# A table of rank offsets for the plan of the attention stage

## The chip, the cores and the metric

The kernel runs on 1 core of a Trainium2 chip. The metric is the device time of one execution in microseconds. The comparison is with the kernel before, whose median of 3 runs is 1107.73 us (1107.68 to 1110.07).

## What is computed

Attention over 2 batches, 8 heads, 576 positions and a head size of 64, then a gated product, then a soft mixture of eight experts, all in float32. Cut to what matters:

```python
q_rot, k_rot = rotate(q), rotate(k)                       # rotary embedding
attn = softmax(q_rot @ k_rot.T / sqrt(64))                # per batch and head
x = (attn @ v)  -> 1152 tokens x 512
x = ((x @ w1) * (x @ w2)) @ w3 @ w_out                    # w3 (1024x1024), w_out (1024x512)
P = sinkhorn(x @ w_gate)                                  # 8 rounds over rows and columns
out = sum over e of P[:, e] * (relu(x @ ew1[e]) @ ew2[e])
```

## The kernel before

Three stages follow each other. **Attention** fills the first 183 us or so; the heads are taken in eight pairs, n = 0 to 7. For each pair the rows of q and k are loaded (`load_qk`, tile `raw`), rotated (`rope_mul`, `rope_add`), cut into a high and a low part (`rope_hi` on ScalarE, `rope_lo`), and spread over partitions by transfers from SBUF to SBUF (`spread_k` into `kk`, `spread_q` into `sq`). Then come nine blocks of scores: four query tiles i = 0 to 3 with a block for each head (`scores`, L351) and one mixed block (`mixed_scores`, L374). A block's row maximum is taken on VectorE (`row_max`, L381), its exponential on ScalarE (`exponentials`, L385), its transposes on TensorE (`transposes`, L399 to L405, three or two groups of up to three), and these are copied from PSUM (`moved`, L418) by VectorE or ScalarE. `norm_columns` (L439, L442) turns the row sums, and `values` (L456) multiplies with v. Scores have two banks of PSUM (psS), transposes two (psT).

In the same stage the matrix product w3 @ w_out is made (`w34_product`, L242 to L244, three matmuls for each of 64 products; `w34_hi` L249 and `w34_lo` L254 take each finished i off its one bank psW). It doesn't depend on attention and fills TensorE where attention leaves it free. Its operands come as 64-bit words by eight loads of w_out (`wo_load`) and sixteen of w3 (`w3_load`, u = 0 to 15) into two buffers `wide`, and are converted in five steps: ScalarE to `cvy` (L193), VectorE shift (L198) and join (L201) to `cvu`, ScalarE high part (L206), and a low part on GpSimd or VectorE (L209). The high and low parts of w3 have two places that take turns. What is left of the 64 products runs behind the last `values`; the last eight (i = 7) are outside the plan.

**The gated product** (`branch`, L153 to L155) begins at 208.23 us, **the experts** run from there to the end in an order of their own plan.

What sets the order in the attention stage is `Plan` (L54). Each step has costs in us for the engines that can run it, a rank, the steps that it needs, and buffers that it takes or frees. `order()` walks a simulated time: among all steps that could start, the one with the lowest rank is issued, on the engine where it is ready. The ranks are written by hand (a pair's time t = n x 18 us, minus 30 for its rope, plus 3.6 for each tile, 1000 for the w34 products). Each engine then runs its list in that order and waits at its head; SyncE issues nearly all transfers. Where the plan leaves TensorE idle by more than some 0.7 us, and no `w34_product` has been issued yet, it emits filler matmuls on `ident` (L635), whose result nobody reads.

Of the kernel before, what the change touches and what calls it, by code (L numbers as in the profile page):

```python
# [19 lines left out]
P = 128  # L20
# [30 lines left out]
QSCALE = D**-0.5  # L51


class Plan:  # L54


# [12 lines left out]
    def step(self, name, costs, rank, run, needs=(), takes=(), frees=(), port=(), paired=False):  # L69


        self.steps[name] = costs, rank, run, list(needs), list(takes), list(frees), port, paired

    def order(self, window=None):
        todo, now, busy = dict(self.steps), 0.0, dict.fromkeys(self.SIGNAL, 0.0)
# [47 lines left out]
def attention_two_moes(ctx: ExitStack, tc: tile.TileContext, rope, qk, v, mw12, mw3t, mwo, wg, ew1, ew2, out):  # L123
# [359 lines left out]
    def step(f, args, costs, rank, needs=(), takes=(), frees=(), **kw):  # L483

        many = f in (rope_mul, rope_add, rope_lo, moved, x_lo)
        plan.step((f, *args), costs, rank, lambda e: f(*args, ENG[e]) if many else f(*args), needs, takes, frees, **kw)
# [9 lines left out]
        plan.step(("tab", c), {"act": 0.1}, -99.0 + c.start / S, lambda e, c=c: act.dma_start(tab[:, :, c], rope[:, :, c]))  # L496
    for n in range(NP):
        t = n * NQ * TILE
        step(load_v, (n,), {"sp": moving(4 * P * (NBLK + 1) * D)}, t - 40.0, takes=[("v", n)])
        ready = []  # L500
        for w in (1, 0):
            pieces = (every,) if n else halves if w else (slice(0, SF), slice(SF, S))
            for c in pieces:
                a, m = (n, w, c), c.stop - c.start
                r = t - 30.0 if n else -50.0 if c.start == 0 or w else -40.0
                r += 2 * (1 - w)
                rot = [("pool", on_pool)] * (n > 0) + [("dve", on_dve)] * (n < 2)
                tk = [("raw", (n, w))] if c.start == 0 else []
                step(load_qk, a, {"sp": moving(8 * P * m)}, t - 30.0 - w if n else -90.0 + c.start / S + 0.1 * (1 - w), takes=tk)
                step(rope_mul, a, {e: f(2 * m) for e, f in rot}, r, [(load_qk, *a), ("tab", halves[0]), ("tab", halves[c.stop > HS])], port=both)  # L510
                step(rope_add, a, {e: f(m) for e, f in rot}, r, [(rope_mul, *a)], port=both)
                tk = [(("sq", "kk")[w], n)] if n else []
                step(rope_hi, a, {"act": act_sb(m)}, r, [(rope_add, *a)], tk)
                fr = [("raw", (n, w))] if n == 0 and c is pieces[-1] else []
                cost = {"pool": on_pool(m)} if n and w else {"dve": on_dve(m)}
                step(rope_lo, a, cost, r, [(rope_hi, *a)], frees=fr, port=both)
            if n == 0:
                ready.append([(rope_lo, 0, w, c) for c in pieces])
                continue
            ready.append([(rope_lo, n, w, every)])  # L520
            for j, x in ((j, x) for j in range(2) for x in range(2)):
                if w:
                    for part, made in enumerate((rope_hi, rope_lo)):
                        step(spread_k, (n, j, x, part), {"sp": moving(4 * D * S)}, t - 30.0, [(made, n, 1, every)], frees=[("raw", (n, 1))])
                        ready[-1].append((spread_k, n, j, x, part))
                else:
                    needs = [((rope_hi, rope_lo)[x], n, 0, every)]
                    step(spread_q, (n, j, x), {"sp": moving(4 * D * S)}, t - 30.0, needs, frees=[("raw", (n, 0))])
                    ready[-1].append((spread_q, n, j, x))
        before = []  # L530
        for i in range(NQ):
            g, k, _ = group(i)
            r = t + i * TILE
            for j in range(2 - (i == MIX)):
                tk = [("psS", (n, i, j))]
                if j == 0:
                    tk += [("e", (n, i)), ("nm", (n, i))] + [("sm", (n, g))] * (k == 0)
                fr = [("kk", n), ("sq", n)] if n and i == MIX else []
                needs = ready[0] + (ready[1] if n or i * P >= SF else ready[1][:1]) + before
                if i < MIX:  # L540
                    made = scores, n, i, j
                    step(scores, (n, i, j), {"pe": 0.53 if n else 0.8}, r + j, needs, tk, fr)
                else:
                    made = mixed_scores, n
                    if n == 0:
                        for q in range(2):
                            step(mix_first, (q,), {"act": 0.2}, r, ready[1])
                        needs = needs + [(mix_first, 0), (mix_first, 1)]
                    step(mixed_scores, (n,), {"pe": 1.14 if n else 1.7}, r + j, needs, tk, fr)
                before = [made]  # L550
                step(row_max, (n, i, j), {"dve": 0.68}, r - 0.1, before)
                fr = [("psS", (n, i, j))] + [("nm", (n, i))] * (j or i == MIX)
                step(exponentials, (n, i, j), {"act": 0.73}, r, [(row_max, n, i, j)], frees=fr)
            r += 6.0
            parts = 3 - (i == MIX)
            for p in range(parts):
                needs = [(exponentials, n, i, min(p, 1) * (i < MIX))] + ([(transposes, n, i, p - 1)] if p else [(transposes, n, i - 1, 0)] if k else [])
                tk = [("psT", (n, i, p))] + ([(f"et{g}", n)] if k == p == 0 else [])
                step(transposes, (n, i, p), {"pe": 0.33}, r, needs, tk, [("e", (n, i))] if p == parts - 1 else [])
                m = 3 * (P if i < MIX else P - HD * p)  # L560
                step(moved, (n, i, p), {"act": act_ps(m), "dve": on_dve(m)}, r, [(transposes, n, i, p)], frees=[("psT", (n, i, p))])
        for g, tiles in enumerate(TILES):
            a, ng = (n, g), (G0, G1)[g]
            r = t + (tiles[-1] + 2.0) * TILE
            needs = [(exponentials, n, i, j) for i in tiles for j in range(2 - (i == MIX))]
            step(norm_sums, a, {"act": 0.2}, r, needs)
            step(norm_rows, a, {"dve": 0.12}, r, [(norm_sums, *a)])
            step(norm_spread, a, {"act": act_sb((4 + g) * D)}, r, [(norm_rows, *a)], [("rb", a)], [("sm", a)])
            step(norm_columns, a, {"pe": (0.24, 0.4)[g]}, r, [(norm_spread, *a)], [("psT", (*a, "r"))], [("rb", a)])
            step(norm_moved, a, {"act": act_ps(ng)}, r, [(norm_columns, *a)], [("r", a)], [("psT", (*a, "r"))])  # L570
            r += 1.1 * TILE
            for m, blocks in enumerate(VPARTS):
                parts = {(i, p) for i in tiles for t in blocks for p in (({0, 2}, {1})[t > 2] if i < MIX else {int(t > 2)})}
                needs = [(moved, n, i, p) for i, p in sorted(parts)] + [(load_v, n)]
                needs += [(values, n, g, m - 1)] if m else []
                last = m == len(VPARTS) - 1
                fr = [(f"et{g}", n)] + [("v", n)] * g if last else []
                step(values, (n, g, m), {"pe": len(blocks) * ng / 600}, r, needs, [("psX", a)] if m == 0 else [], fr, paired=True)
            step(x_scale, a, {"dve": on_dve(ng)}, r, [(values, n, g, len(VPARTS) - 1), (norm_moved, *a)], [("xs", a)], [("psX", a), ("r", a)])
            step(x_hi, a, {"act": act_sb(ng)}, r, [(x_scale, *a)])  # L580
            step(x_lo, a, {"pool": on_pool(ng), "dve": on_dve(ng)}, r, [(x_hi, *a)], frees=[("xs", a)], port=both)

    def wide_steps(load, u, got, rank, takes):

        step(load, (u,), {"sp": moving(8 * P * WU)}, rank - 20.0, takes=[("wide", (load, u))])

        parts = (
            ({"act": 0.57}, (), ["cvy"], ["wide"], ()),
            ({"dve": 0.37}, (), ["cvu"], ["wide"], both),
            ({"dve": 0.63}, (0, 1), [], ["cvy"], both),  # L590
            ({"act": act_sb(WU)}, (2,), [], [], ()),
            ({"pool": on_pool(WU), "dve": on_dve(WU)}, (3,), [], ["cvu"], both),
        )
        for k, (cost, before, tk, fr, port) in enumerate(parts):
            needs = [(load, u)] + [(load, u, p) for p in before]
            tk, fr = ([(p, (load, u)) for p in ps] for ps in (tk, fr))
            tk += takes if k == 3 else []
            plan.step((load, u, k), cost, rank, lambda e, k=k: got[u][2][k](*[ENG[e]][: k == 4]), needs, tk, fr, port)
# [806 lines left out]
```

## Time and profile before

| | us |
|---|---|
| median of 3 runs | 1107.73 (1107.68 to 1110.07) |
| the profiled execution, time | 1109.31 |
| its span, first to last instruction | 1107.5 |
| TensorE busy in the span | 1093.8 (99%) |
| VectorE, ScalarE, GpSimd busy | 797.7, 672.7, 323.2 |
| start of the gated product | 208.23 |

A busy TensorE isn't a TensorE that does needed work: the fillers are counted as busy. Between the span and the time of the same execution lie 1.81 us.

### The profile page before, as it was taken

The numbers are of one execution on the slowest core, as the hardware profiler recorded it, in microseconds if no ns is written. First come the engines' busy times: TensorE is split into PE (matmuls) and PEld (weight loads), VectorE is DVE, ScalarE is ACT, GpSimd is POOL, SyncE is SP. The second block draws the span as 40 slices with busy tenths as digits, with TensorE's granted clock in tenths as the row PEclk, the third lists the DMA queues.
The fourth block names the chain that finished last, engine by engine and source line by source line (L and its number), as shares of the span: only waits on it lengthen the run. The fifth ranks groups of instructions, "written<-read, shape, count | busy, mean of one in ns | idle before, by whom it ended". The sixth has DMA issues, their size and how long they took to land.

```text
span 1107.5 us, 21133 instructions
## 1 busy us (share of the span) xinstructions
PE 1093.8 (99%) x8185; PEld 1039.0 (94%) x8185; DVE 797.7 (72%) x1377; ACT 672.7 (61%) x1393; POOL 323.2 (29%) x289
## 2 busy tenths in 40 slices
PE   8999999999999999999999999999999999999998
PEld 7777777899999999999999999999999999999998
DVE  7887765854433688777876777778776787777876
ACT  5877775643322545667666666666656666666663
POOL 1656441000010101334333333324333333333311
PEclk9999999999999999999999999999999999999999
DMA  7776751530040435787878788778888688787824
GB/s 245 240 231 193 234 166 58 195 129 20 20 118 13 109 96 112 156 181 151 191 155 171 164 172 179 166 150 181 173 163 179 140 188 178 157 184 141 188 37 115
DMA packets 86308, 167.20 MB, mean 151 GB/s; under 512 B 9536, under 2 KB 50240, under 8 KB 86208
## 3 DMA queue, kind: packets, MB, share of 16 engines
q0 software_dynamic: 47632, 55.33, 32.1%
q1 hardware_dynamic: 38032, 109.94, 32.0%
q8 instruction: 64, 1.05, 0.4%
q10 hardware_dynamic: 544, 0.59, 0.2%
q14 instruction: 36, 0.29, 0.1%
HBM read 112.02 MB, written 2.36 MB: 103 GB/s over the span
## 4 chain that ended last, share of the span: by engine, by line
PE 79%; DVE 2%; DMA 0%; ACT 0%; issue 0%; DVEq 0%; SPq 0%
PE T L878 6%; PE T L880 6%; PE T L879 6%; PE zT L984 5%; PE zT L985 5%; PE zT L986 5%; PE s L153 3%; PE s L155 3%; PE s L154 3%; PE Q L878 3%; PE Q L880 3%; PE Q L879 3%; PE zQ L984 3%; PE zQ L986 3%; PE zQ L985 3%; PE A L878 2%
## 5 line engine op out<-in xcount | busy, mean ns | idle before, releaser
L752 POOL DMA_DIRECT2D sums<-sums x92 | 93.9, 1020 | 246.3 <-DMA sums<-sums 90.0
L1035 POOL DMA_DIRECT2D acc<-ztmp x87 | 107.0, 1233 | 134.4 <-ACT ztmp L1032 65.9
L984 PE MATMUL zT<-f,hf 128*128 128x256 f32 x496 | 141.1, 284 | 0.0
L985 PE MATMUL zT<-f,hf 128*128 128x256 f32 x496 | 140.3, 283 | 0.0
L986 PE MATMUL zT<-f,hf 128*128 128x256 f32 x496 | 140.3, 283 | 0.0
L752 POOL DMA_DIRECT2D sums<-in_ew_dram x46 | 41.0, 891 | 270.6 <-issue 119.1
L984 PEld LDWEIGHTS zT<-f,hf 128*128 128x128 f32 x496 | 94.8, 191 | 0.6
L986 PEld LDWEIGHTS zT<-f,hf 128*128 128x128 f32 x496 | 95.2, 192 | 0.0
L985 PEld LDWEIGHTS zT<-f,hf 128*128 128x128 f32 x496 | 94.9, 191 | 0.0
L148 DVE SCALAR_TENSOR_TENSOR y<-y 128x512 f32<-128x512 f32 x128 | 88.0, 687 | 2.3
L878 PE MATMUL T<-x,w 128*128 128x320 f32 x256 | 81.0, 316 | 0.0
L920 ACT ACTIVATE hf<-y 128x512 fp32r<-128x512 f32 x128 | 78.1, 631 | 2.7 <-DVE y L148 2.6
L148 DVE SCALAR_TENSOR_TENSOR hf<-y,hf 128x512 fp32r<-128x512 f32 x96 | 64.8, 686 | 20.2 <-ACT hf L918 20.1
L1032 ACT ACTIVATE ztmp<-ztmp,pr 128x256 f32<-128x256 f32 x174 | 78.6, 500 | 1.1 <-DVE ztmp L145 0.6
L880 PE MATMUL T<-x,w 128*128 128x320 f32 x256 | 79.1, 309 | 0.0
L879 PE MATMUL T<-x,w 128*128 128x320 f32 x256 | 79.0, 309 | 0.0
L918 ACT ACTIVATE hf<-y 128x512 fp32r<-128x512 f32 x96 | 60.1, 627 | 29.9 <-DVE y L889 25.7
L153 PE MATMUL s<-x,w 128*128 128x320 f32 (+1 forms) x256 | 76.2, 298 | 0.7 <-DVE gf L680 0.7
L155 PE MATMUL s<-x,w 128*128 128x320 f32 (+1 forms) x256 | 75.8, 296 | 0.0
L154 PE MATMUL s<-x,w 128*128 128x320 f32 (+1 forms) x256 | 75.8, 296 | 0.0
L878 PE MATMUL T<-y,w 128*128 128x256 f32 x256 | 72.5, 283 | 0.0
L880 PE MATMUL T<-y,w 128*128 128x256 f32 x256 | 72.4, 283 | 0.0
(308 smaller groups left out, 3695.6 us busy)
## 6 DMA issues: line engine op xcount, KB each, us to landing
sums<-in_ew_dram SPq DMA_DIRECT2D x62, 512.0 KB, 4.3
acc<-ztmp POOLq DMA_DIRECT2D x87, 256.0 KB, 5.6
wide<-in_ew_dram SPq DMA_DIRECT2D x34, 512.0 KB, 3.9
wide<-in_ew_dram SPq DMA_DIRECT2D x30, 384.0 KB, 5.2
wide<-in_mw3t_dram SPq DMA_DIRECT2D x16, 512.0 KB, 5.0
wide<-in_mw_dram SPq DMA_DIRECT2D x16, 512.0 KB, 3.2
sums<-in_ew_dram POOLq DMA_DIRECT2D x16, 512.0 KB, 6.5
sums<-sums POOLq DMA_DIRECT2D x32, 256.0 KB, 5.7
```

The lines of the kernel that those rows point to most:

```text
L148: dve.scalar_tensor_tensor(out=dst, in0=a, scalar=0.0, in1=b, op0=ALU.max, op1=op)
L153: pe.matmul(ps, wh, xh, start=(i == 0), stop=False)
L154: pe.matmul(ps, wh, xl, start=False, stop=False)
L155: pe.matmul(ps, wl, xh, start=False, stop=(i == n - 1))
L752: pool.dma_start(dst, src, accum_op=ALU.add)
L878: pe.matmul(ps, h[:, ws], x[0], start=(first and k == 0), stop=False, **kw)
L879: pe.matmul(ps, h[:, ws], x[1], start=False, stop=False, **kw)
L880: pe.matmul(ps, l[:, ws], x[0], start=False, stop=(k == 1), **kw)
L984: pe.matmul(ps[:, t], h, wh[:, u], start=(opens and u == 0), stop=False, **kw)
L985: pe.matmul(ps[:, t], h, wl[:, u], start=False, stop=False, **kw)
L986: pe.matmul(ps[:, t], l, wh[:, u], start=False, stop=(u == 1), **kw)
L1035: pool.dma_start(block(q, b, d), ztmp[:, slot(q, src)], accum_op=ALU.add)
```

## The change

A table `EARLIER` gives an offset for each kind of step and each pair n (or unit u); `Plan.step` adds it to the rank. Steps of the experts' plan have names that begin with a string and get none. The offsets are large against the hand-written ranks (up to some 2000), so inside what is ready they set a new order. The offsets come from a search over the plan itself, with durations scattered at random. Four added needs make buffers that are picked by number (`v`, the places of w3, `kk`, and the high parts of rope) be written in turn.

```diff
+EARLIER = dict(
+    scores=(-313, -222.5, -156.2, -1208.1, -593.3, -148.2, 765.3, 822.3,),
+    w34_product=(-626, 170.7, 528, -91.5, 296.2, 309.9, 683.5, 450.1, 404.3, -1426.6, -635, -452.7, 2110.7, -827.1,),
...
+def offset(name):
+    if isinstance(name[0], str):
+        return 0.0
+    f = name[0].__name__
+    i = name[1] if isinstance(name[1], int) else 0
...
+    return EARLIER.get(f, (0.0,) * (i + 1))[i]
...
-        self.steps[name] = costs, rank, run, list(needs), list(takes), list(frees), port, paired
+        self.steps[name] = costs, rank + offset(name), run, list(needs), list(takes), list(frees), port, paired
...
-        step(load_v, (n,), {"sp": moving(4 * P * (NBLK + 1) * D)}, t - 40.0, takes=[("v", n)])
+        step(load_v, (n,), {"sp": moving(4 * P * (NBLK + 1) * D)}, t - 40.0, [(load_v, n - 1)] if n else [], [("v", n)])
...
-                step(rope_hi, a, {"act": act_sb(m)}, r, [(rope_add, *a)], tk)
+                step(rope_hi, a, {"act": act_sb(m)}, r, [(rope_add, *a)] + ([(rope_hi, n - 1, w, every)] if n > 1 else []), tk)
...
+                        needs = [(made, n, 1, every)] + ([(spread_k, n - 1, 0, 0, 0)] if n > 1 else [])
...
+            needs = [(load, u)] + [(load, u, p) for p in before] + ([(load, u - 1, 3)] if takes and k == 3 and u else [])
```

No instruction of the needed work is added or removed. Line numbers of the changed kernel are higher by 43 or 44 (L399 is L442 there, L242 is L285, L635 is L679). From the gated product on, every engine has the same list in both kernels. In the attention stage the lists differ on all engines; the filler matmuls (L635) go from 48 to 41, of which the first 37 stand at the same places. Copies of transposes go from 59 on VectorE and 53 on ScalarE to 51 and 61. Of the 192 matmuls of the w34 products, 96 stood ahead of the last `values` and 111 do now.

TensorE, behind the mixed block (L374) of pair 2; before:

```order
L374 MATMUL s<-kk,sq_93 128x64
L399 MATMUL t<-ident,e 128x128 x6
L635 MATMUL w_105<-ident 128x128
L399 MATMUL t<-ident,e 128x128 x3
L635 MATMUL w_105<-ident 128x128 x5
L402 MATMUL t<-ident,e 128x128 x4
L405 MATMUL t<-ident,e 64x64 x2
L351 MATMUL s<-kk,sq_94 128x288 x8
```

TensorE at the same place, now:

```order
L417 MATMUL s<-kk,sq_93 128x64
L442 MATMUL t<-ident,e 128x128 x6
L285 MATMUL w_828<-y_85,y_86 128x512
L286 MATMUL w_828<-y_85,y_86 128x512
L287 MATMUL w_828<-y_85,y_86 128x512
...
L442 MATMUL t<-ident,e 128x128 x3
L394 MATMUL s<-kk,sq_94 128x288 x8
L445 MATMUL t<-ident,e 128x128 x4
L448 MATMUL t<-ident,e 64x64 x2
```

Six filler calls have gone and two w34 products (six matmuls, the row of dots is the second) stand in their place; the scores of pair 3 have moved ahead of the transposes of the mixed block.

VectorE, where the one bank of the w34 products is handed from one i to the next with the fewest TensorE instructions between; before, at pair 5, `keep` is the low part that frees the bank, `s` are scores, `t` transposes:

```order
L418 COPY et0_1554<-t_1587 128x3x128
L418 COPY et0_1554<-t_1593 128x3x128
L381 TENSOR_REDUCE nm_1600<-s_1602 128x1
L418 COPY et0_1554<-t_1615 128x3x128
L381 TENSOR_REDUCE nm_1600<-s_1624 128x1
L254 TENSOR_TENSOR keep_1632<-w34_1315,keep_1631 128x512
L418 COPY et0_1554<-t_1634 128x3x128
```

VectorE, the shortest such place now, at pair 3:

```order
L424 TENSOR_REDUCE nm_1117<-s_1118 128x1
L424 TENSOR_REDUCE nm_1117<-s_1127 128x1
L461 COPY et1_1155<-t_1162 128x3x128
L461 COPY et1_1155<-t_1171 128x3x128
L297 TENSOR_TENSOR keep_1177<-w34_828,keep_1176 128x512
L241 TENSOR_SCALAR cvu_1202<-wide_1124 128x512
L424 TENSOR_REDUCE nm_1180<-s_1181 128x1
```

The row maximum that stood between the copy and the low part now stands behind it. On TensorE, three transposes, four score matmuls and six transposes lay between the two products; now it is three transposes, a mixed block of ten matmuls and six transposes.

SyncE, the transfers ahead of the scores of pair 3 (`sq` is the query block), before:

```order
L322 DMA kk_800<-raw_656 64x576 x8
L312 DMA sq1_94<-raw_689 64x576
L314 DMA sq1_94<-raw_689 64x512
L315 DMA sq1_94<-raw_689 64x64
...
L180 DMA wide_911<-in_mwo_dram 128x1024
L180 DMA wide_927<-in_mw3t_dram 128x1024
```

SyncE, the same transfers now:

```order
L365 DMA kk_699<-raw_558 64x576 x8
L318 DMA raw_770<-in_qk_dram 128x1152
L355 DMA sq1_94<-raw_621 64x576 x2
L322 DMA v1_96<-in_v_dram 128x640
L223 DMA wide_825<-in_mw3t_dram 128x1024
L223 DMA wide_856<-in_mwo_dram 128x1024
L357 DMA sq1_94<-raw_621 64x512
L358 DMA sq1_94<-raw_621 64x64
```

Two loads into `wide` and one of v, which stood outside the six transfers of the query block, now stand between the first two and the last four. At pair 4 one such load stands between the first three and the last three.

## Rows read from the trace of the kernel before

**Rows 1.** The page, part 1: busy us (share), instructions of each engine.

```profile
PE 1093.8 (99%) x8185; PEld 1039.0 (94%) x8185; DVE 797.7 (72%) x1377; ACT 672.7 (61%) x1393; POOL 323.2 (29%) x289
```

**Rows 2.** Windows: stretch, its length, each engine's busy us (instructions), granted clock, DMA share, GB/s.

```profile
31.00:90.00 59.00, 56.99 (x434) 44.59 (x435) 47.76 (x86) 45.83 (x114) 37.31 (x23) 1.00 0.70 221
90.00:182.00 92.00, 89.31 (x638) 69.98 (x637) 66.90 (x121) 67.51 (x168) 36.43 (x22) 1.00 0.59 173
182.00:210.00 28.00, 27.38 (x135) 21.32 (x134) 17.73 (x30) 14.30 (x27) 5.27 (x4) 1.00 0.45 156
...
240.00:1107.00 867.00, 863.07 (x6581) 850.56 (x6579) 618.92 (x1058) 509.72 (x1010) 237.75 (x225) 1.00 0.66 140
```

**Rows 3.** Waits of TensorE, 31 to 210 us: total us, times, longest.

```profile
PE s L351 <- ACT e L385: 1.6, 4, 0.7
PE t L399 <- ACT et L418: 1.5, 4, 0.7
PE w L242 <- DVE keep L254: 0.7, 1, 0.7
PE t L244 <- POOL y L209: 0.6, 1, 0.6
PE t L402 <- ACT e L385: 0.4, 1, 0.4
PE t L399 <- DVE et L418: 0.3, 1, 0.3
PE s L351 <- DMA sq<-raw: 0.2, 1, 0.2
```

**Rows 4.** Timeline of TensorE, the fillers after 31 us: start, us, what [idle before].

```profile
31.80 0.39 PE L635 MATMUL w<-ident 128*128 128x128 f32 x2
32.53 0.79 PE L351 MATMUL s<-kk,sq 128*128 128x288 f32 x4 [0.34 <-ACT e L385]
...
51.93 0.49 PE L635 MATMUL w<-ident 128*128 128x128 f32 x2
52.72 0.80 PE L351 MATMUL s<-kk,sq 128*128 128x288 f32 x4 [0.30 <-ACT e L385]
...
60.39 0.83 PE L635 MATMUL w<-ident 128*128 128x128 f32 x6
61.51 0.55 PE L399 MATMUL t<-ident,e 128*128 128x128 f32 x3 [0.29 <-DVE et L418]
61.92 0.80 PE L351 MATMUL s<-kk,sq 128*128 128x288 f32 x4
...
68.63 0.39 PE L635 MATMUL w<-ident 128*128 128x128 f32 x2
...
69.42 1.28 PE L635 MATMUL w<-ident 128*128 128x128 f32 x10
71.05 0.66 PE L402 MATMUL t<-ident,e 128*128 128x128 f32 x4 [0.35 <-ACT e L385]
```

**Rows 5.** Timeline of TensorE, third group of nine transposes in a row, pair 3.

```profile
91.19 0.55 PE L399 MATMUL t<-ident,e 128*128 128x128 f32 x3 [0.75 <-ACT et L418]
```

**Rows 6.** Timelines of TensorE and VectorE at the bank's handover, pair 5.

```profile
126.11 0.49 PE L399 MATMUL t<-ident,e 128*128 128x128 f32 x3
126.35 0.78 PE L351 MATMUL s<-kk,sq 128*128 128x288 f32 x4
126.97 0.87 PE L399 MATMUL t<-ident,e 128*128 128x128 f32 x6
128.58 0.50 PE L242 MATMUL w<-y,y 128*128 128x512 f32 x1 [0.73 <-DVE keep L254]
...
127.17 0.76 DVE L381 TENSOR_REDUCE nm<-s 128x1 f32<-128x576 f32 x1
127.84 0.68 DVE L254 TENSOR_TENSOR keep<-w,keep 128x512 fp32r<-128x512 f32 x1
```

**Rows 7.** Waits of SyncE's queue, 31 to 180 us, for a free buffer `wide`.

```profile
SPq L180 <- DVE cvu L198: 29.2, 4, 18.2
```

More of the change, by code (lines that the diff above doesn't have):

```diff
@@ L51 @@
 QSCALE = D**-0.5
+EARLIER = dict(
+    tab=(-331.3,),
+    load_v=(-354.5, -305.2, -333.7, -395.2, -443.9, 51.4, 117.2, 192.7,),
+    load_qk=(-446.5, -563.6, -504.3, -521.9, -370.4, -480.6, -321.4, -369.9, -103.5, -302.6, 278.6, 84.4, 472.6, 406.8, 467.4, 843,),
+    rope=(1321.6, -520.9, -134.3, -274.1, 194.8, 7.4, -158.9, -290.5, 328.6, -520.8, 143.6, 402.5, 347.5, 45.1, 180.4, -275.3,),
+    scores=(-313, -222.5, -156.2, -1208.1, -593.3, -148.2, 765.3, 822.3,),
+    row_max=(95, -339.3, -459.3, -371.5, 64.3, 242.1, -463.7, -503.3,),
+    exponentials=(384.2, -538.1, 789.4, -718.7, -632.5, -1318, 348.2, 645.8,),
+    transposes=(-134.9, -177.4, 112.9, -358.7, 215.6, 0.5, -1059.9, 358.7,),
+    moved=(1394.8, 286.6, 336.9, 12.6, 714.3, 298.7, 466.7, -1387.4,),
+    mix_first=(-949.3, -113.9,),
+    norm=(-843.9, 97.1, -780.5, 228, 118.6, -417.2, 4.4, 254.9,),
+    values=(-4.2, -86.4, 299.7, -497.7, 853.3, -376, 637.5, -708.8,),
+    x=(441.7, 1706.3, 185.6, 172.7, -875.5, -366.6, -560.4, 537.3,),
+    spread_k=(0, -556.8, 314.7, 1368.1, 1907, -52.9, 495, 1430.1,),
+    spread_q=(0, -415.3, 170, 455.1, -1105.8, 404.2, 0.2, -420.3,),
+    wo_load_load=(-186.6, -86, -265.2, -203.6, -195.1, -52.4, 29.5, -0.3,),
+    wo_load_conv=(58.2, 32.3, 1384.4, 986.9, 305.7, 156.8, -525.6, 70.7,),
+    w3_load_load=(-91.6, -111.5, -106.8, 11.1, 110.4, 22.1, 125.3, 117.8, 177.5, 105.1, 183.8, 169.1, 196.4, 187.5, 579.5, 1319.7,),
+    w3_load_conv=(326.6, 480.6, 997.2, -330.1, -865.3, 1165.5, 467.8, 612, -414.8, 87.8, 536.1, 58.2, 444.8, 772, -487.8, 358.1,),
+    w34_product=(-626, 170.7, 528, -91.5, 296.2, 309.9, 683.5, 450.1, 404.3, -1426.6, -635, -452.7, 2110.7, -827.1,),
+    w34_hi=(-260.6, -1009.8, 557.3, 262.6, 450.5, 215.9, 1078.5,),
+    w34_lo=(1307, 625.5, -825.9, -437.9, 169.5, 1350.3, 101.1,),
+)
@@ new lines, in offset @@
+def offset(name):
[3 more added lines that the diff above has]
+    i = name[1] if isinstance(name[1], int) else 0
+    if f in ("load_qk", "rope_mul", "rope_add", "rope_hi", "rope_lo", "head_hi", "head_lo"):
+        i = 2 * i + name[2]
+    elif f in ("wo_load", "w3_load"):
+        f += "_load" if len(name) == 2 else "_conv"
+    for stem in ("norm", "rope", "head", "x"):
+        if f.startswith(stem + "_"):
+            f = stem
+    f = {"mixed_scores": "scores"}.get(f, f)
+    return EARLIER.get(f, (0.0,) * (i + 1))[i]
@@ L523, in attention_two_moes @@
                     for part, made in enumerate((rope_hi, rope_lo)):
-                        step(spread_k, (n, j, x, part), {"sp": moving(4 * D * S)}, t - 30.0, [(made, n, 1, every)], frees=[("raw", (n, 1))])
+                        needs = [(made, n, 1, every)] + ([(spread_k, n - 1, 0, 0, 0)] if n > 1 else [])
+                        step(spread_k, (n, j, x, part), {"sp": moving(4 * D * S)}, t - 30.0, needs, frees=[("raw", (n, 1))])
                         ready[-1].append((spread_k, n, j, x, part))
@@ L594, in wide_steps @@
         for k, (cost, before, tk, fr, port) in enumerate(parts):
-            needs = [(load, u)] + [(load, u, p) for p in before]
+            needs = [(load, u)] + [(load, u, p) for p in before] + ([(load, u - 1, 3)] if takes and k == 3 and u else [])
             tk, fr = ([(p, (load, u)) for p in ps] for ps in (tk, fr))
```

## The prediction

> **What bounds the kernel now.** I read the page's busy times first. TensorE is busy 99% of the span and every other engine at most 72% [rows 1], so only what TensorE does or waits for can move the end. Next the busy times by stage. From 240 us on TensorE is busy 863.07 of 867 us [rows 2]; that part has the same lists in both kernels, and so has the gated product ahead of it, so the change can act on the attention stage alone. There TensorE is busy 56.99 of 59 us, 89.31 of 92 and 27.38 of 28 [rows 2]: 5.3 us of idle time after 31 us. The list of its waits names them [rows 3], and they add up to the same 5.3. But busy is not needed: the timeline shows five groups of fillers after 31 us, 0.39, 0.49, 0.83, 0.39 and 1.28 us, 3.4 in all (each call is two passes, so x2 is one call) [rows 4]. What a better order can win after 31 us is therefore 5.3 + 3.4 = 8.7 us, 0.8% of the time. Ahead of 31 us the fillers stand at the same places in both orders and the first scores wait for the same loads; I count nothing there.
>
> The other limit is how fast softmax hands on. From 31 to 90 us VectorE is busy 47.76 and ScalarE 45.83 of 59 us, 81 and 78% [rows 2]; TensorE waits there mostly for exponentials and for copies of transposes, and both are behind other work on those two engines. From 90 us on w34 products fill the gaps, and the idle share falls only from 3.4 to 2.9%.
>
> **The change part by part.** *Fillers.* After 31 us there were eleven calls for 3.4 us. Now there are four: three together (as at 60.39, 0.83) and one (0.39 to 0.49) [rows 4], about 1.2. That takes 2.2 us off TensorE, if the gap has gone and not only its filling. The first fence shows why it may be so: where 0.39 + 1.28 us of fillers ran behind pair 2, two w34 products now run, work that must be done anyway. In all 15 more of the w34 matmuls stand ahead of the last `values`; at 27.38 / 135 = 0.2 us each [rows 2] that is 3 us that the end of the stage no longer needs. It is the same gain seen from the other side and isn't counted again. Ends: 0 (the gaps stay as waits; from the first w34 product on the plan emits no fillers, and that point has moved from pair 3 to pair 2, so gaps in pair 2 don't show in the order) and -2.2.
>
> *Waits beside the fillers.* Four of the five groups are followed by a wait, since the real gap was longer than the planned one: 0.34, 0.30, 0.29 and 0.35, together 1.3 [rows 4]. Two groups of fillers are left, at 0.3 each: 0.6. That is -0.7; ends -1.3 and 0.
>
> *Handover of the bank psW.* At 128.58 TensorE waited 0.73 us for the low part that frees the bank. VectorE began that part at 127.84, behind a row maximum that began at 127.17 [rows 6]. In the new order the row maximum stands behind it, 0.67 us won. And TensorE comes later: before, three transposes (0.24, 126.11 to 126.35), four score matmuls (0.62) and six transposes (0.88, up to 127.85, where the wait begins); now ten score matmuls stand in place of the four, at 0.62 / 4 each some 1.5 us, so 0.9 later. 1.6 us against a wait of 0.73: it goes, -0.7. Ends: -0.7 and 0 (ScalarE's high part, which must come first, isn't fixed by this). Late next is the next product's own operands, and the low part of the next w3 unit is on VectorE behind the same row maximum.
>
> *Nine transposes in a row.* The banks for transposes are two, so the third group of three waits for a copy. There are four such places, and the four waits for a copy by ScalarE are theirs: 1.5 us in all, the longest 0.75 in pair 3 [rows 3, 5]. In the new order three are left, and in pair 3 two w34 products stand behind the first six transposes. I take -0.75 for it; ends -0.75 and 0.
>
> *More changes between kinds of matmul.* TensorE's list changes kind 216 times up to the gated product and not 199, mostly because six transposes have become twice three. Three took 0.24 us at 126.11 and 0.41 at 61.51, six 0.88 at 126.97 [rows 4, 6], so two threes are no dearer than a six. Two groups of eight score matmuls become four and four; for these I take the difference of the two threes, 0.17 each: +0.3. Ends: 0 and 17 x 0.17 = 2.9.
>
> *Copies.* Eight of 112 copies of transposes go from VectorE to ScalarE, the less busy of the two in the first half [rows 2]. That relieves the engine that holds the row maxima; hidden in the fifth of the time that both have free. 0; if ScalarE's cover is gone, it shows in the waits for exponentials (1.6 us now [rows 3]).
>
> *The end of the stage.* TensorE waited 0.6 us there for a low part of w3 on GpSimd [rows 3]. Four w3 loads are left for it and not five, but the run of products is also 3 us shorter, and ScalarE now takes the first step of the second load of w1 ahead of the last w3 unit's high part. I leave the 0.6 as it is; ends 0 and 2. The gated product's first weights come behind it on the same queues and are needed only when these products are done.
>
> *The added needs.* They name steps that come earlier in a pair's own chain. What is queued behind a waiting one is told in the SyncE rival; 0 in the sum.
>
> Sum: -2.2 - 0.7 - 0.7 - 0.75 + 0.3 = -4.05 us. The profiled execution took 1109.31 us with 1.81 outside its span; it lies 1.6 us (0.14%) above the median, and the difference is made on the median: 1107.73 - 4.05 = **1103.7 us**. Measurements of this kernel tell about 0.3% from no change, here 3.3 us, so the border of faster is 1104.4.
>
> **The rivals.** *The waits come back.* The order was searched in the plan's own time, and in the kernel before the real stage was already 1.3 us slower than that time beside the fillers alone. If the gaps in pairs 2 to 5 are merely unfilled, the terms of fillers and their waits (2.9) vanish and 1.2 is left: 1106.6. For it: VectorE and ScalarE at some 80%, with a longer list of other work on them. Against it: 15 more needed matmuls stand ahead of the last `values`, which a plan with the same gaps couldn't place there.
>
> *SyncE holds back the query block (slower).* A transfer that waits for its buffer holds all behind it. In the kernel before, SyncE waited 29.2 us in four waits for a free `wide` between 31 and 180 us, 18.2 the longest [rows 7], but these loads stood outside the transfers of a query block. Even so the scores of pair 4 waited 0.2 us for their query block [rows 3], so there was no lead left there. Now two such loads stand ahead of four transfers of pair 3's block, and one ahead of three of pair 4's. By the mean wait, 29.2 / 4 = 7.3 us, each place could lose up to that: one place gives 1103.7 + 7.3 = 1111.0, both 1118. It decides from 7.3 us in all, where slower begins (1111.1). Against it: the conversion that frees the first of those buffers stands on VectorE right behind the low part from which that query block itself is made, so the wait should be an instruction or two long.
>
> [...]
>
> *The change does nothing*: excluded for the order, which differs on every engine; a time that stays all the same is in the first rival.
>
> **How the numbers follow.** The forecast, faster by over 0.3%: 0.50 (some 0.05 of it below 1100, where waits that I left standing go too). The waits come back, or one place on SyncE loses a few us, or the clock (0.02): within 0.3%, 0.34. Slower, the query block in two places or a wait that I don't see: 0.16. Range: the lower end is the whole of what can be won, 8.7, so 1099.0; below it I leave hardly anything. Above, the within cases reach 1111; up to 1110 some 0.17 is left out.
>
> **What would show it.** Fillers after 31 us for some 1.2 us and no L635 beyond pair 2; no wait of a w34 product for `keep`; no wait over 0.5 us for a copy; the gated product beginning at about 208.2 - 4.05 = 204.2 us; the stretch from there to the end as long as before. [...]

## The result, and the profile after

The changed kernel takes **1117.88 us** (median of 6 runs, 1114.54 to 1118.9) against 1108.09 for the kernel before on the same chip: ratio 1.0078, 95% interval 1.0067 to 1.0089. It is slower by 0.8%, about 9 us; the forecast was 1103.7, and its range ended at 1110.0.

The profiled execution of the changed kernel is the fastest of the six, 1114.54 us with a span of 1112.7. Its windows, with the columns of [rows 2]:

```profile
31.00:90.00 59.00, 51.83 (x360) 38.67 (x361) 40.85 (x73) 42.06 (x104) 36.98 (x23) 0.97 0.76 218
90.00:182.00 92.00, 90.21 (x658) 71.04 (x657) 66.73 (x118) 68.60 (x170) 41.14 (x26) 1.00 0.60 170
182.00:210.00 28.00, 28.00 (x153) 21.64 (x149) 17.28 (x32) 15.78 (x35) 2.04 (x2) 1.00 0.41 137
...
240.00:1107.00 867.00, 866.78 (x6606) 854.33 (x6605) 620.67 (x1063) 512.28 (x1016) 237.45 (x225) 1.00 0.65 139
```

From 90 to 210 us TensorE is idle for 1.8 us; before it was 3.3 [rows 2]. In size that part went as forecast. The loss is in the first line: 7.2 us idle where it was 2.0 [rows 2], and a granted clock of 0.97. TensorE's waits from 31 to 210 us, which answer to [rows 3]:

```profile
PE t L442 <- ACT et L461: 2.1, 4, 1.2
PE t L482 <- ACT et L461: 2.0, 1, 2.0
PE s L394 <- ACT e L428: 1.8, 3, 1.3
PE t L442 <- ACT r L490: 1.4, 1, 1.4
PE s L394 <- DMA sq<-raw: 0.5, 1, 0.5
```

Nearly all (7.6 of 8.6 us) are for ScalarE, so ask what ScalarE waited for. These are its timeline, GpSimd's and TensorE's at the longest wait (start, us, what, [idle before]):

```profile
53.96 0.21 ACT L465 ACTIVATE sm<-sm 128x5 f32<-128x5 f32 x1
57.18 0.68 ACT L340 ACTIVATE raw<-raw 128x576 fp32r<-128x576 f32 x1 [3.02 <-POOL raw L330]
57.77 0.46 ACT L461 COPY et<-t 128x384 f32<-128x384 f32 x1
58.13 0.74 ACT L428 ACTIVATE e<-s,nm 128x576 f32<-128x576 f32 x1
...
53.04 2.64 POOL L326 TENSOR_TENSOR raw<-raw,tab 128x1152 f32<-128x1152 f32 x1 [4.79 <-DMA raw<-in_qk_dram]
55.75 1.40 POOL L330 TENSOR_TENSOR raw<-raw 128x576 f32<-128x576 f32 x1
...
58.29 0.44 PE L482 MATMUL t<-ident,rb 128*128 128x128 f32 x2 [2.04 <-ACT et L461]
59.02 1.18 PE L394 MATMUL s<-kk,sq 128*128 128x288 f32 x4 [0.30 <-ACT e L428]
```

Read it upwards. TensorE waits for a copy of transposes; the copy stands on ScalarE behind `rope_hi` of pair 3 (L340); that waits for GpSimd's rope, and GpSimd had waited 4.79 us for the load of pair 3's k into `raw`. So the last question goes to SyncE, which issued that load. Its timeline there:

```profile
39.21 4.49 SPq L365 DMA_DIRECT2D kk<-raw  x5
48.15 0.33 SPq L318 DMA_DIRECT2D raw<-in_qk_dram  x1
48.54 1.10 SPq L355 DMA_DIRECT2D sq<-raw  x2
...
51.64 0.60 SPq L358 DMA_DIRECT2D sq<-raw  x1
54.95 0.33 SPq L318 DMA_DIRECT2D raw<-in_qk_dram  x1
55.33 0.91 SPq L223 DMA_DIRECT2D wide<-in_mw3t_dram  x2
```

Between 43.70 and 48.15 SyncE issues nothing: the load of k stands right behind the eight transfers out of the buffer that it is to fill, and these must have landed first. The query block (`sq`) is issued 4.5 us later for it. The same happens again behind the query block (52.24 to 54.95), with two loads into `wide` behind that. In SyncE's waits up to 190 us the changed kernel has these lines for its `raw` loads, and the kernel before the last one:

```profile
SPq L318 <- DMA sq<-raw: 19.9, 8, 4.7
SPq L318 <- DMA kk<-raw: 18.5, 16, 3.7
...
SPq L275 <- DMA sq<-raw: 1.9, 4, 0.7
```

38.4 us against 1.9. Issuing isn't landing; these are the medians from issue to landing of the transfers out of `raw`, first before, then now:

```profile
kk<-raw SPq DMA_DIRECT2D x56, 144.0 KB, 2.5
sq<-raw SPq DMA_DIRECT2D x14, 144.0 KB, 2.4
...
kk<-raw SPq DMA_DIRECT2D x56, 144.0 KB, 4.6
sq<-raw SPq DMA_DIRECT2D x14, 144.0 KB, 4.9
```

The gap of 4.45 us from 43.70 to 48.15 is of that size. It holds back more than the query block. ScalarE's longest waits from 31 to 120 us, in sum, are for loads into `wide`:

```profile
ACT cvy L236 <- DMA wide<-in_mw3t_dram: 5.4, 4, 2.5
...
ACT cvy L236 <- DMA wide<-in_mwo_dram: 3.0, 1, 3.0
```

Before, these waits were 2.0 us in all. The one of 3.0 us ends at 40.53; its load was issued at 33.82, right behind a `raw` load that had itself waited 2.55 us, and TensorE waits 1.30 us for an exponential that stands behind it (42.34).

Behind the hole TensorE's granted clock fell to 0.50, for 3.4 us in all:

```profile
59.00:60.00 1.00, 0.98 (x5) 0.97 (x6) 0.00 (x0) 1.00 (x4) 0.75 (x1) 0.61 0.86 329
60.00:61.00 1.00, 1.00 (x6) 1.00 (x5) 0.76 (x2) 0.31 (x1) 0.82 (x1) 0.50 0.97 384
61.00:62.00 1.00, 1.00 (x6) 0.98 (x5) 0.62 (x2) 0.46 (x1) 1.00 (x1) 0.50 1.08 261
62.00:63.00 1.00, 1.00 (x9) 0.66 (x7) 1.00 (x3) 0.94 (x3) 0.92 (x2) 0.68 1.05 238
```

The matmuls slowed: three transposes took 0.84 us at 60.00 and 0.49 at 63.34, four score matmuls 1.31 at 60.49 and 0.78 at 63.58. Counted by the clock, 0.39 + 0.50 + 0.50 + 0.32 = 1.7 us of TensorE's work were lost, an estimate that takes the work to slow with the granted clock. The gated product begins at 212.46 us, 4.2 later than in the profile before.

### The profile page after: what moved, and what is told of

Read it like the earlier page. It is cut to its first block, busy times and chain, and to the rows that moved or that the text cites. A ratio compares the mean times of both kernels' runs of the same rounds, so it can differ in the third digit from the quotient of the medians.

```text
span 1112.7 us, 21130 instructions
## 1 busy us (share of the span) xinstructions
PE 1094.8 (98%) x8171; PEld 1038.9 (93%) x8171; DVE 792.7 (71%) x1368; ACT 675.5 (61%) x1401; POOL 322.8 (29%) x290
## 4 chain that ended last, share of the span: by engine, by line
PE 88%; DMA 6%; DVE 3%; ACT 1%; issue 1%; SPq 0%; POOL 0%; ACTq 0%; DVEq 0%
PE T L922 6%; PE T L924 6%; PE T L923 6%; PE zT L1028 5%; PE zT L1029 5%; PE zT L1030 5%; PE s L196 3%; PE s L197 3%; PE s L198 3%; PE Q L922 3%; PE Q L924 3%; PE Q L923 3%; PE zQ L1028 3%; PE zQ L1030 3%; PE zQ L1029 3%; PE x L499 2%
## 5 line engine op out<-in xcount | busy, mean ns | idle before, releaser
L191 DVE SCALAR_TENSOR_TENSOR hf<-y,hf 128x512 fp32r<-128x512 f32 x96 | 64.7, 685 | 20.6 <-ACT hf L962 20.5
```

The lines of the kernel that those rows point to most:

```text
L191: dve.scalar_tensor_tensor(out=dst, in0=a, scalar=0.0, in1=b, op0=ALU.max, op1=op)
```

## Experiments

Two theories stood against each other. **Landing**: the new order puts the `raw` loads where they must wait for a landing, and all the rest follows. **Heads**: the new lists of ScalarE and VectorE are too tight, whatever SyncE does. Ratios are against the kernel before on the same chip, with 95% intervals.

**A third buffer.** All lists stay; only the buffer that the load waits for is another one.

```diff
-            raw[n, w] = att_p.tile([P, 2, S], F32, name="raw", bufs=2)
+            raw[n, w] = att_p.tile([P, 2, S], F32, name="raw", bufs=3)
```

> The changed kernel with three buffers `raw` in place of two; every engine's list stays as it is. Theory L (landing): the changed order puts the next pair's `raw` load on SyncE right behind the transfers that free its buffer, and it waits for their landing (38.4 us of such waits in the profile of the changed kernel, 18.6 of them between 31 and 90 us, against 1.9 before); all that is queued behind it comes late. With a third buffer these waits fall under 5 us, the 3.0 us hole of ScalarE at 54 to 57 us shrinks below 1 us, the gated product begins at 204 to 207 us, and the time is 1104 to 1109. Rival H (heads): the lists of ScalarE and VectorE are themselves too tight, whatever SyncE does: the waits on SyncE go and the time stays at 1114 to 1119. [...]

Measured: 1109.76 us (10 runs, 1106.35 to 1117.04), ratio 1.0016 (0.9994 to 1.0038). SyncE's waits for the landing of `kk` and `sq` are gone from its `raw` loads, ScalarE's hole ahead of `rope_hi` and its waits for `wide` too, and the gated product begins at 207.23. Most of the loss was the landing. But the order is no faster than before, ScalarE has another hole of 3.54 us (51.83, ahead of L249, for a join on VectorE), and the scatter is wide; the two slowest runs, 1116.76 and 1117.04, are those with the lowest mean granted clock, 0.992 and 0.993.

> Control: the kernel before with three buffers `raw`, lists unchanged. Theory L: only 1.9 us of SyncE's waits were for a landing there, so 1106 to 1110, no change that can be measured. If a third buffer is worth something for another reason (places in memory, an earlier load), 3 us or more come off here as well, and the gain of the changed kernel with three buffers says less.

Measured: 1109.22 us, ratio 1.0001 (0.9991 to 1.0011). The third buffer is worth nothing by itself. The gated product begins at 206.39 us in this profile and at 208.23 in that of the kernel before, with the same lists: single profiles of one order differ by some 2 us.

**SyncE's order alone, both ways.** In the kernel before, the load of k goes ahead of the query block, for pairs 2 to 6 (the changed kernel has a sixth such place, with the load of pair 7's q):

```diff
+        for n in range(2, 7):
+            q = next(k for k, x in enumerate(steps) if x[0][:3] == (load_qk, n, 1))
+            moved_step = steps.pop(q)
+            k = next(k for k, x in enumerate(steps) if x[0][:2] == (spread_q, n - 1))
+            steps.insert(k, moved_step)
```

> The kernel before with one move: for pairs 2 to 6 the load of k into `raw` goes ahead of the six transfers of the query block of the pair before, where the changed kernel has it. All other lists stay those of before. Theory L: each of the five loads waits 2 to 4.5 us for the landing of the eight transfers into `kk` (10 to 20 us in all on SyncE), the query blocks come as much later, and the kernel is slower: 1110 to 1117. Rival H: ScalarE's and VectorE's lists are those of before, so 1107 to 1110.

Measured: 1128.56 us, ratio 1.0172 (1.0151 to 1.0192), more than expected. SyncE's loads wait 20.6 us there, and the price is seen on TensorE:

```profile
PE s L351 <- DMA sq<-raw: 12.1, 5, 3.4
```

Five pairs begin late by up to 3.4 us, and the clock is 0.91 from 31 to 90 us and 0.96 from 90 to 182. With a third buffer in this kernel:

> The kernel before with the load of k ahead of the query block for pairs 2 to 6, as in the run that took 1128.6 us, now with three buffers `raw`. Theory L (the load waits for a landing and holds what is behind it): with a third buffer nothing is left to wait for, the 20.6 us of waits for `kk` and `sq` on SyncE go, and with them nearly all of the loss: 1107 to 1111. Rival E (engines): the query block comes late because 576 KB of the load are ahead of it in the same DMA engines; then TensorE still waits some 8 to 12 us for `sq`: 1115 to 1125.

Measured: 1116.52 us, ratio 1.0067 (1.0050 to 1.0084): 12 of the 20 us come back, 8 don't. The landing theory alone is too small. TensorE still waits 4.8 us for `sq`, though SyncE's `raw` loads no longer wait for a landing of `kk` or `sq`. What is left shows in the median from issue to landing of the same 144 KB transfers, first before, then here:

```profile
sq<-raw SPq DMA_DIRECT2D x14, 144.0 KB, 2.4
...
sq<-raw SPq DMA_DIRECT2D x14, 144.0 KB, 4.3
```

With two buffers and the load at the same place the median is 4.1 us, so it isn't the buffer but the place of the load, 576 KB issued just ahead of them, that makes them land later. That they share the DMA engines with it, as rival E has it, fits, but no run shows it. So the new place of the load has two prices: a wait on SyncE, which a buffer takes away, and a slower landing of what follows, which it doesn't.

In the changed kernel the order of before on SyncE (the query block whole, the loads behind it):

```diff
+        for n in range(2, 8):
+            late = [x for x in steps if x[0][:2] == (spread_q, n - 1)]
+            q = steps.index(late[0])
+            late += [x for x in steps[:q] if x[0][:2] == (load_qk, n)]
+            steps = [x for x in steps if x not in late]
+            k = next(k for k, x in enumerate(steps) if x[0][:3] == (rope_lo, n - 1, 0))
+            steps[k + 1 : k + 1] = late
```

> The changed kernel with SyncE's order of before in one point: the six transfers of a query block stand together right behind the eight of `kk`, and the next pair's loads into `raw` behind them. The other lists stay changed. Theory L: waits of the loads for `kk` fall from 18.5 us to some 2, the query blocks come 2 to 4 us earlier, but the rope of the next pair, which ScalarE's new list wants early, gets its load no earlier than now; so a part comes back: 1108 to 1115. Rival H: 1115 to 1119.

Measured: 1132.44 us, ratio 1.0218 (1.0201 to 1.0235). My expectation was wrong: not a part comes back, but some 15.5 us are added ((1.0218 - 1.0078) x 1108). ScalarE's waits from 31 to 120 us say why; first here, then in the changed kernel:

```profile
ACT raw L340 <- POOL raw L330: 7.3, 2, 5.9
...
ACT raw L340 <- POOL raw L330: 3.8, 2, 3.0
```

The new ScalarE list needs the early load: ahead of the wait of 5.9 us GpSimd had waited 5.82 for the load of pair 5's k, which SyncE issued at 100.34 us and not at 90.38 as in the changed kernel. The lists of the engines are one order; here a piece of the old one in the new one was worse than either. So "heads" looks less like a rival than like the other half: the heads are only as good as the loads that they count on.

**The start.** The four loads of pair 0 and their rope steps stand in another order (both halves of k first). In the changed kernel with three buffers TensorE had run out of fillers by then, and its clock, at 1.00 until then, fell (timeline, then windows):

```profile
11.09 1.33 PE L394 MATMUL s<-x 64*128 64x288 f32 x7 [1.69 <-ACT x L340]
...
11.00:14.00 3.00, 2.91 (x15) 2.58 (x16) 2.46 (x6) 1.29 (x5) 0.00 (x0) 0.65 0.98 341
14.00:17.00 3.00, 3.00 (x22) 2.61 (x22) 1.31 (x3) 1.91 (x5) 0.00 (x0) 0.78 0.39 131
```

In the kernel before, with the start of the changed one (`first` is the changed kernel's order of these twenty steps):

```diff
+        at_first = [k for k, x in enumerate(steps) if x[0] in first]
+        by_name = {x[0]: x for x in steps}
+        for k, name in zip(at_first, first):
+            steps[k] = by_name[name]
```

> The kernel before with the changed kernel's order of pair 0's four loads and of their rope steps (both halves of k ahead of both pieces of q) on SyncE, VectorE and ScalarE; all behind the first scores as before. Theory S (start): the second half of k needs the second half of the table, which lands 0.75 us later than what VectorE takes there in the kernel before (its wait is 1.75 us in the profile of the changed kernel against 1.00), so the first scores begin 0.6 us later and the time is 0.6 us longer, and more where TensorE has run out of fillers and its clock falls: 1109 to 1112. Rival N (nothing there): 1108.5 to 1109.5, as the step that I counted at nothing.

Measured: 1109.67 us, ratio 1.0013 (1.0004 to 1.0022): 1.5 us. The first scores begin at 10.66 us, before at 10.15, but the gated product at 207.70, before at 208.23; TensorE's wait for the gated product's `gf` on VectorE is 1.3 us (0.7 before). So the order at the start costs the 1.5 us; where they are lost, beyond the first 0.5, these two profiles don't show. In the changed kernel with the start of before:

> The changed kernel (two buffers `raw`) with the start of before alone. [...] Rival: the late start is what makes the later holes, since all later lists run behind it; then most of the 9 us come back: 1108 to 1112.

Measured: 1118.63 us, ratio 1.0095 (1.0078 to 1.0112). Nothing comes back while the landing waits stand (40.2 us on SyncE here), though the first scores begin at 9.71 us and not at 10.75. That is above the 1115 to 1117.5 that I expected if the two causes add up, and above the rival's range; that the waits hide the 1.5 us is the likely reading. Both causes away, a third buffer and the start of before:

> The changed kernel with three buffers `raw` and the start of before (order of pair 0's loads and rope steps). If the landing waits and the start are the two causes, this is the searched order without both: first scores at 10.0 to 10.3 us and not 11.1, clock 1.00 from 10 to 31 us, gated product at 205 to 206.5 us, time 1105 to 1108 with less scatter than the 1106 to 1117 of three buffers alone. If the scatter is from the waits of the conversions (two joins on VectorE took 3.1 us and not 0.7 beside a GpSimd product), it stays: 1106 to 1117, median 1109.

> The same kernel without the two moves, once more beside it on the same chip: 1107 to 1109, and in its profile one long join and one long low part again if these collisions are fixed by the order, other ones if they are chance.

Measured: 1108.12 us (12 runs, 1105.86 to 1110.57), ratio 1.0000 (0.9990 to 1.0010), and once more 1108.01, ratio 0.9998 (0.9989 to 1.0007). The scatter is less than half of that with three buffers alone. In the first profile the gated product begins at 204.72 us, nearly the 204.2 that I had forecast for the change, in the second at 209.04, behind a hole of 2.37 us at 52 us and a clock of 0.94 from 31 to 60; and the median doesn't move. Three things can take the gain. One is the stretch behind: from the gated product to the end of the span it is 900.4 us in the first profile (1105.1 - 204.72), before 899.3 (1107.5 - 208.23); TensorE waits there 1.6 us for VectorE's `gf` (0.7 before). But all thirteen profiles here have the same lists in that stretch, and it takes 899.1 to 901.8 us in them, so one pair of profiles says little. The second is the clock: in 8 of the 24 timed runs the mean granted clock is 0.998 or 0.997, and these take 1108.98 to 1111.67, the other 16 1105.86 to 1109.37; the runs of before beside them are at 0.999 or 1.000. The second profile, with the hole, is of one of the eight (1111.53). The third is VectorE beside GpSimd; timelines of GpSimd, VectorE and TensorE:

```profile
46.95 2.64 POOL L326 TENSOR_TENSOR raw<-raw,tab 128x1152 f32<-128x1152 f32 x1 [1.33 <-DMA raw<-in_qk_dram]
...
46.53 0.42 DVE L241 TENSOR_SCALAR cvu<-wide 128x512 int32<-128x512 int32 x1
46.98 3.16 DVE L244 SCALAR_TENSOR_TENSOR cvu<-cvy,cvu 128x512 int32<-128x512 int32 x1
50.06 0.75 DVE L424 TENSOR_REDUCE nm<-s 128x1 f32<-128x576 f32 x1
...
51.23 0.93 PE L442 MATMUL t<-ident,e 128*128 128x128 f32 x6 [1.27 <-ACT et L461]
```

The join takes 3.16 us and not 0.69, since GpSimd's product began 0.03 us ahead of it; the row maximum and, over ScalarE, TensorE wait. The join ends at 50.14, 0.55 us behind the product's end at 49.59, as if it had done its work only then. The plan lets the two engines take turns as well, but in its own time the join comes first and the product begins as it ends. In the second profile the product began at 46.40 us, as its load had landed, and held the shift instead (2.88 us and not 0.42, the join 1.77): that made the hole of 2.37. TensorE's one wait for `rb`, 1.38 us behind a low part of 2.92 in the first profile, is 1.3 us again. So the order sets the meeting, and half a microsecond in a load's landing sets what it costs.

**Two moves on VectorE.** The join, and a low part of 2.9 us of the same kind at 136 us, go behind the row maxima (`behind(a, b)` puts the steps a right behind step b in the order):

```diff
+        behind([(wo_load, 4, 1), (wo_load, 4, 2)], (row_max, 1, 4, 0))
+        behind([(wo_load, 4, 3)], (exponentials, 1, 4, 0))
+        behind([(rope_lo, 7, 0, every), (spread_q, 7, 0, 1), (spread_q, 7, 1, 1)], (row_max, 6, 0, 1))
```

> Three buffers `raw`, the start of before, and two moves: on VectorE a shift and a join of a w_out unit (`wo_load` 4) go behind the row maximum of pair 1's mixed block, with the high part on ScalarE behind its exponential; and the low part of the rope of pair 7's q goes behind two row maxima of pair 6, with the two transfers that need it. In the profile of the kernel without these moves the join took 3.16 us and the low part 2.9, where others of their kind take 0.7, each beside a GpSimd product of 2.65 us, and TensorE waited 1.27 and 1.38 us for what stood behind them. Theory P (a VectorE step beside a GpSimd product is held until that ends, with all that stands behind it): both waits go, 2.6 us, so the time is 1104 to 1106. Rival: TensorE then waits for something else, since these engines are full anyway: 1107 to 1109.

Measured: 1106.94 us (11 runs), ratio 0.9986 (0.9978 to 0.9995), 1.1 us under the kernel without the moves beside it, where the two intervals overlap. It is the only version whose interval lies below the kernel before: by 1.5 us, less than expected and just under the rival's range. The second wait is gone. At the first the join stands behind the row maximum and still meets the next GpSimd step (1.79 us), and TensorE waits 1.5 us for a copy behind it.

**Another search.** A new table was searched against a model in which a transfer frees its buffer 2 us behind its end and VectorE and GpSimd hold each other up (the 2 us are my estimate; before, the medians from issue to landing of the transfers out of `raw` are 1.9 to 2.5); three buffers, start of before.

```diff
-    scores=(-313, -222.5, -156.2, -1208.1, -593.3, -148.2, 765.3, 822.3,),
+    scores=(-3.9, -20.9, 78, 0, 153.1, 338.5, -5.2, 0,),
...
```

> Three buffers `raw`, the start of before, and another table of offsets, searched against a model of the queues in which a transfer frees its buffer only some 2 us behind its end, and in which VectorE and GpSimd hold up each other in the order in which they come. If the missing landing in the plan was the cause of the loss, and not a search by itself, this order keeps on the chip what it promises: TensorE's idle time and fillers after 31 us under 5 us in place of 8.7, the gated product at 200 to 204 us, time 1101 to 1105. If any order found by search loses its gain to what no model has (clock, scatter of the transfers): 1107 to 1112.

Measured: 1114.14 us (10 runs, 1107.50 to 1117.49), ratio 1.0045 (1.0027 to 1.0064). Windows:

```profile
34.00:41.00 7.00, 6.41 (x33) 4.58 (x34) 3.36 (x7) 4.12 (x11) 0.13 (x1) 0.55 0.03 11
...
57.00:66.00 9.00, 8.08 (x45) 5.82 (x45) 5.84 (x10) 6.81 (x17) 3.98 (x3) 0.62 0.35 115
...
75.00:182.00 107.00, 106.45 (x770) 83.68 (x770) 82.61 (x144) 80.72 (x199) 53.48 (x35) 1.00 0.68 193
```

From 75 to 182 us TensorE is idle for 0.55 us, far less than in any other kernel here. No `raw` load waits for a landing of `kk` or `sq` any more. But ahead of 75 us VectorE still meets GpSimd: two collisions make a hole of 3.65 us, two more one of 1.82, and behind both the granted clock is low, 0.55 from 34 to 41 us and 0.62 from 57 to 66: 0.45 x 6.41 + 0.38 x 8.08 = 6 us lost to the clock alone, by the estimate above. A better model of landing wasn't enough. One meeting in this profile went the other way round, with the join first:

```profile
50.71 3.19 POOL L325 TENSOR_TENSOR raw<-raw,tab 128x1152 f32<-128x1152 f32 x1 [2.24 <-DMA raw<-in_qk_dram]
...
50.68 0.69 DVE L243 SCALAR_TENSOR_TENSOR cvu<-cvy,cvu 128x512 int32<-128x512 int32 x1
```

There the join keeps its 0.69 us, and the product takes 3.19 and not 2.64.

## Why the prediction was wrong

**The step that failed** is the SyncE part of the change. The order of SyncE that I showed has, at pair 3, the row `raw_770` between `kk` and `sq`, and right above it `kk_699<-raw_558`; there are six such places, at pairs 1 to 6. I priced the two loads into `wide` further down, and this load at nothing. I should have asked which buffer the load takes: one of two, and the one that those very transfers read. The bound was in the trace of before: 2.5 us from issue to landing for a transfer into `kk`, six times, is some 15 us on a queue on which I had noted that no lead was left. Measured were 18.5 us, and 19.9 more for the loads that wait for `sq` in the same way (1.9 before). The plan made the same mistake, and its code says so: in `order()` the end of a step counts at once for the engine that issued it, and for the others 3.0 us later if SyncE issued it (`SIGNAL`). In its time a load right behind SyncE's own transfers waits for nothing.

The rival that should have held the loss shared a chance of 0.16 with a wait that I didn't see. It had half of the mechanism: a transfer that waits for its buffer holds all behind it (nothing is issued from 43.70 to 48.15), at some 7 us a place. It had the wrong buffer, the wrong pairs and the wrong victim: no score group of pair 3 or 4 waits over 1 us for `sq` (the one wait is 0.5 us, in pair 2). What came too late for TensorE was what ScalarE needs, the next pair's k over GpSimd and the loads into `wide`. In the kernel before with the load moved, TensorE waited for `sq` itself, as the rival says.

In the two profiles the stage's loss adds up like this: 5.2 us more idle time from 31 to 90, 1.7 for the clock there, 0.6 for later first scores (10.75 against 10.15), less 2.1 of fillers and 1.5 of idle time from 90 to 210: 3.9 of the 4.2. Their spans lie 5.2 us apart and the medians 9.8, so this sum explains about half of the loss.

**Fillers** (-2.2) and **their waits** (-0.7): the fillers came as told, 1.3 us left after 31 us and none after 64. The waits didn't shrink, they grew to new ones; the term rested on the gaps being planned, and the plan was wrong about what ends them. **Handover** (-0.7): right, no w34 product waits for `keep`. **Nine transposes in a row** (-0.75): wrong, the waits of these transposes for copies by ScalarE are 2.1 us (1.5 before); the longest, 1.2, comes behind a ScalarE that had waited 2.52 us for a load into `wide`. **More changes of kind** (+0.3): nothing here shows it apart. **Copies** (0): not tested apart. TensorE's waits for ScalarE's copies did grow, to 4.1 us, and the two longest of them come behind late inputs. **End of the stage** (0.6 left): better than told, TensorE is busy all of 182 to 210 us. **"I count nothing" ahead of 31 us**: wrong by 1.5 us, shown in the kernel before; not seen in the changed one. **The stretch behind as long as before**: 900.2 us in the changed kernel (1112.7 - 212.46), before 899.3, inside the spread of the thirteen profiles.

**The clock** (0.02): that chance was my estimate, and no run shows the fall that it stands for, with the fillers gone and needed products in their place: in the changed kernel no filler runs after 64 us, and the clock is 1.00 from 63 to 210. It did fall, to 0.97 from 31 to 90 us, behind a hole. Some holes of TensorE, with the granted clock around or behind them:

| profile | hole, us (ends at) | granted clock (window) |
|---|---|---|
| changed kernel | 2.04 (58.29) | 0.50 (60 to 62) |
| | 1.38 (69.81) | 1.00 (69 to 75) |
| start of before alone | 1.97 (56.12) | 0.90 (45 to 60) |
| | 1.64 (68.48) | 0.99 (60 to 75) |
| | 2.38 (104.00) | 0.89 (105 to 120) |
| both causes away, second | 2.37 (52.22) | 0.57 (52 to 56) |
| two moves | 1.54 (52.78) | 0.85 (52 to 56), 0.72 (56 to 60) |
| another search | 3.65 (34.59) | 0.50 (34 to 40) |
| | 1.82 (56.66) | 0.50 (58 to 64) |
| before, load moved | 2.15 (53.21) | 0.77 (45 to 60) |
| | 2.25 (80.07) | 0.89 (75 to 90) |
| before, load moved, three buffers | 1.49 (102.41) | 1.00 (90 to 182) |

Needed products have taken the fillers' place, but in a hole no product runs either.

With the two causes away the stage is as short as forecast in one profile (204.72 us) and not in the other (209.04), and the lists of before reach 206.39 in one. So it isn't shown that the sum of the stage was right for an order whose loads come when the plan thinks; the one hit may be luck. Nor do I know why the median of the changed kernel lies 3 us above its profiled run, whose mean granted clock (0.997) lies among those of the other five (0.994 to 1.000). In the one with the start of before, whose profiled run took 1119.92 us, there are more holes of the same kind (a wait of 2.4 us at 104 us, the clock at 0.94 from 90 to 120).

## What to carry to other kernels

When a load moves on a queue, ask which buffer it takes and what is issued last out of that buffer: if that is right ahead of it, the load waits for the landing and everything behind it on the queue waits too (here 38.4 us of such waits against 1.9), and even with a spare buffer what follows a large load can land late (here 4.3 us from issue to landing and not 2.4, behind 576 KB). A plan that counts a step on the same queue as done when it is issued will seek out that place. And an order that is tight on every engine is only as good as its latest input: price it by one load that comes 3 us late (ScalarE's hole here was 3.02).

## Not expected of the hardware

Two holes cost more than their length: the one of 2.04 us was followed by 3.4 us at a granted clock of 0.50 (1.7 us lost, by the estimate above), the one of 3.65 us by 7 us at 0.55 (2.9 lost). And 0.03 us stand between two outcomes for a VectorE join beside a GpSimd product: begun 0.03 us behind the product it took 3.16 us, begun 0.03 us ahead of one it took 0.69, and the product 3.19 and not 2.64.
